# Attention, routed experts and a gated layer in one kernel: the hand-written order also places loads, stores and table reads, and gate stores and decoding move

## The chip, the core and the metric

The kernel runs on one core of a Trainium2 chip. Its engines have queues of their own and run side by side: TensorE (PE; its weight loads are listed as PEld), VectorE (DVE), ScalarE (ACT), GpSimd (POOL) and SyncE (SP), which here only reads table entries and issues DMA transfers. Each engine works through its own instructions in the order in which the program names them; between engines only semaphores hold. The metric is the device time of one execution, in microseconds (us), as the median of several runs.

## What is computed

```python
# attention without a softmax, per batch and head (8 batches, 8 heads, 576 tokens, 64 wide)
kv = einsum('bhsd,bhse->bhde', k, v)
out = einsum('bhsd,bhde->bhse', q, kv)
x = out / sqrt(mean(out * out) + 1e-06) * g_norm       # -> 4608 tokens of 512
# one of 8 experts for each token
logits = x @ w_gate + modality_bias[modality_id]
e_idx, gate_w = argmax(logits), softmax(logits)[e_idx]
x[mask_e] = gate_w * (relu(x[mask_e] @ w1[e]) @ w2[e]) # w1: 512 x 1024, w2: 1024 x 512
# a gated layer; its three weights are given in float64
out = (sigmoid(x @ w_gate2) * (x @ w_val)) @ w_out     # 512 -> 1536 -> 512
```

## The kernel before

**Stages.** First attention, batch by batch (`for b in range(B)`, each with row groups `r` = 0 to 4), which also finds each token's expert; then the expert stage; then the gated layer. Products are made of float32 values split into two parts (`h` for the high part, made by ScalarE, `l` for the rest, made by VectorE), three matmuls for one.

**Attention.** In step (b, r) `emit_out(b - 1, r)` multiplies queries by `kv` on TensorE; ScalarE copies the result out and squares it, VectorE sums the squares (`ssq`). `norm(b - 2)` (L532) makes norms and logits, mostly on VectorE. `choose` (L557) takes the best expert for a pair of batches, `rank` (L573) counts each token's place among its expert's, with ten small matmuls (`rkp`), `lanes` (L603) makes a one-hot table `lo`, `numbers` (L610) multiplies it by token numbers into `lid`: nine activations on ScalarE, or one product on VectorE or GpSimd. Batch 6 is `early`: then `front_items` (L635) reads from the first half of the tokens which two experts have full pairs of tiles (a small matmul `tote`, then some fifteen VectorE operations into `est0`). At b = 7 `front_rows` (L662) finds the row numbers of these two items (VectorE's `se`, 36 small matmuls `phe`, two VectorE operations into `gidx0`) and four indirect gathers on GpSimd fetch their rows.

**Items.** The expert stage works on items of 256 tokens of one expert: items 0 and 1 (`NFRONT` = 2) still inside attention's end, items 2 to 21 in `run`, L1139. An item has four steps j: B(j) is x times a quarter of `w1` (24 matmuls of 256 columns), `h` the relu, D(j) is `h` times a quarter of `w2` (12 matmuls of 512 columns; for items 0 and 1 and odd j 8 matmuls in plain float32, L332).

**The explicit order.** Between attention's loop and `run` stands `ORDER` (L897), a list of names; the program calls `todo[name]()` one after another, which fixes every engine's own sequence. The names: `out0`..`out4` the last batch's products, `o`, `sq`, `ssq` their copies, squares and sums; `n6a n6s n6b`, `n7a n7s n7b` the norms; `S5 S6 S7` the stores of `x` for the last batches, on SP; `rk2p rk2`, `rk3p rk3` ranks, `ln` lanes, `nu2a` and so on numbers (nine activations each); `ch3` the last choice; `totp tot sega segb slots soh php gidx` the tables of all rows (`soh` on VectorE, `php` 72 small matmuls on TensorE, `gidx` the row numbers); `exp` the table of experts `est`; `plx` the exponentials of the logits for the gate (VectorE's difference, ScalarE's Exp with its table load, L832); `plc pld` the scatter's row numbers; `g0 g1` the gathers for items 2 and 3; `nx`, `A`, `xh`, `xl` the norm, transposes and split of gathered rows, by item and tile (`A20` is item 2, tile 0); `w1h4 w1l4`, `w2h4 w2l4` weight splits; `B4`, `h4`, `hl4`, `D4` the products of step 4, which is item 1, j = 0; `L1_j` and `L2_j` the loads of item 1's quarters of `w1` and `w2`; `y0 y1` the results of items 0 and 1.

Item 0, item 1 and item 2 use the same buffer `half0`, so a quarter is loaded for the next item when the split, or the plain D, of the one before has read it. Items 2 and on are loaded only if the expert differs from the one in the buffer; SP reads expert and flag from `est` (L173, L174):

```python
exp=lambda: (experts(), read_item(NFRONT), read_item(NFRONT + 1))
behind = [(f"w1l{NJ1 + j}", j, 0) for j in range(NJ1)] + ...   # item 2's loads, each after the name that frees it
```

**The loop.** `run` walks the 80 steps of items 2 to 21: products, the splits and loads for the items ahead, and beside them `decode`: 28 units of the gated layer's float64 weights, each loaded raw (`d_raw`, 512 KB), and some steps later turned into float32 by ScalarE (`d_e`, L133) and VectorE and stored. Before, unit i was loaded at step 13 i // 6 + 3, its exponent taken two steps later, its store four steps later. `store_gate` (L1075) stores one number for each token to DRAM, in four transfers of runs of four numbers or one; it was called at step 0.

Of the kernel before, what the change touches and what calls it, by code (L numbers as in the profile page):

```python
# [10 lines left out]
F32 = mybir.dt.float32  # L11
# [73 lines left out]
def attention_moe_glu_kernel(  # L85
# [270 lines left out]
    with ExitStack() as st:  # L356
# [250 lines left out]
            lo = lo_t[bp] = wk.tile(bc, BF16, tag="lo", name="lo", bufs=1)  # L607
            nc.vector.tensor_tensor(out=lo, in0=iotab.unsqueeze(1).broadcast_to(bc), in1=lane.unsqueeze(2).broadcast_to(bc), op=ALU.is_equal)

        def numbers(bp, eng, ws=(0, 1)):  # L610

            t0, n, bc, lo = 9 * bp, 9, [128, 9, 128], lo_t[bp]
            for w in ws:
                c = w * NTILE + t0
                if eng is nc.scalar:
                    for t in range(n):
                        nc.scalar.activation(out=lid[:, t0 + t, w, :], in_=lo[:, t, :], func=ACTF.Copy, scale=ct[:, C_TOK + c + t:C_TOK + c + t + 1])
                else:
                    eng.tensor_tensor(out=lid[:, t0:t0 + n, w, :], in0=lo, in1=tokb[:, c:c + n].unsqueeze(2).broadcast_to(bc), op=ALU.mult)
# [74 lines left out]
        for b in range(B):  # L694
            if b < B:
                qc = wk.tile([128, 4, H, D], F32, tag="qc", name="qc", bufs=1)
                nc.scalar.activation(out=qc[:, 0], in_=q_t[b][:, :, 0, :], func=ACTF.Copy)
                emit_kv(b)
            if b == 2:
                make_bias()  # L700
            for r in range(5):
                if b < B and r == 0:
                    nc.scalar.activation(out=qc[:, 1], in_=q_t[b][:, :, 1, :], func=ACTF.Copy)
                    for i in (2, 3):
                        nc.gpsimd.tensor_copy(out=qc[:, i], in_=q_t[b][:, :, i, :])
                if b:
                    emit_out(b - 1, r)
                if b < B:
                    if r == 0:
                        emit_RT(b)  # L710
                    if r < 4:
                        emit_qT((b, r), qc[:, r].rearrange("p h d -> p (h d)"))
                    if b % 2 and r == (4 if b < B - 1 else 0):
                        emit_qT((b, 4), qr_t[b // 2].rearrange("p h d -> p (h d)"))
                    if r == 2:
                        emit_M(b)
                if r == 1:
                    load_kv(b + 2)
                    load_q(b + 2)
                    if b == 0:  # L720
                        load_mod()
                    for i in {5: (1,), 6: (0, 3, 2)}.get(b, ()):
                        store_x(i)
                early = b == B - 2
                if (b, r) in ((4, 1), (5, 4)):
                    rank(b - 4)
                if (b, r) in ((4, 3), (6, 0)):
                    lanes(b // 2 - 2)
                if (b, r) == (4, 3):
                    numbers(0, nc.gpsimd)  # L730
                if early and r == 1:
                    numbers(1, nc.scalar, (0,))
                    numbers(1, nc.vector, (1,))
                if 1 < b < B and r == (2 if early else 1):
                    norm(b - 2)
                if b % 2 and b > 1 and r == 3:
                    choose(b // 2 - 1)
                if early and r == 3:
                    front_items()
                if b == B - 1:  # L740
                    if r == 0:
                        front_rows()
                        for t in range(NFRONT):
                            gather(t)
                    if r == 1:
                        for t in range(NFRONT):
                            read_item(t)
                        ld_scope.close()
                        mw = [mw_scope.enter_context(tc.tile_pool(name="m_wr0", bufs=1, side="right", reuse_waits="tile"))]
                        w1p = w1_scope.enter_context(tc.tile_pool(name="m_w1", bufs=3, side="right", reuse_waits="tile"))  # L750
                        half0 = mw[0].tile([128, 2, KC * F1], F32, tag="half0", name="half0")
                        w1r.append(half0[:, 0].rearrange("p (c f) -> p c f", f=F1))
                        w2r.append(half0[:, 1].rearrange("p (c f) -> p c f", f=DM))
                        for j in range(NJ1):
                            load_w(0, j, 0)
                            load_w(0, j, 1)
                    if r == 4:
                        store_x(B - 4)
# [60 lines left out]
        def experts():  # L819
            nc.vector.tensor_reduce(out=esf[:, 0:NITEM], in_=cmp[0:1], op=ALU.add, axis=AX)  # L820
            nc.vector.tensor_scalar(out=ehi, in0=esf[:, 0:NITEM], scalar1=-1.0, scalar2=float(2 * E), op0=ALU.mult, op1=ALU.add)
            nc.vector.tensor_tensor(out=esf[:, 0:NITEM], in0=esf[:, 0:NITEM], in1=ehi, op=ALU.min)
            nc.vector.tensor_scalar(out=esf[:, 0:NITEM], in0=esf[:, 0:NITEM], scalar1=float(E - 1), scalar2=0.0, op0=ALU.min, op1=ALU.max)
            nc.vector.memset(esf[:, NITEM:NITEM + NFRONT + 2], 1.0)
            nc.vector.tensor_tensor(out=esf[:, NITEM + NFRONT:NITEM + NFRONT + 1], in0=esf[:, NFRONT:NFRONT + 1], in1=front.ep[0:1, 1:2], op=ALU.not_equal)
            nc.vector.tensor_tensor(out=esf[:, NITEM + NFRONT + 2:2 * NITEM], in0=esf[:, NFRONT + 2:NITEM], in1=esf[:, NFRONT:NITEM - 2], op=ALU.not_equal)
            nc.vector.tensor_copy(out=esf[:, 2 * NITEM:], in_=seg[0:1, 17:18])
            nc.vector.tensor_copy(out=est, in_=esf)
# [55 lines left out]
        for bp in (2, 3):  # L884
            steps(f"rk{bp}p rk{bp}", rank_parts(bp))
            todo[f"ln{bp}"] = lambda bp=bp: lanes(bp)
            for w in range(2):
# [4 lines left out]
        steps("plc pld", places())  # L892
        place(ch3=lambda: choose(3), slots=slots, plx=exps, y0=lambda: emit_y(0), y1=lambda: emit_y(1),
              g0=lambda: gather(NFRONT, (0,)), g1=lambda: (gather(NFRONT, (1,)), gather(NFRONT + 1)),
              exp=lambda: (experts(), read_item(NFRONT), read_item(NFRONT + 1)))
        behind = [(f"w1l{NJ1 + j}", j, 0) for j in range(NJ1)] + [(("D" if plain(1, j) else "w2l") + str(NJ1 + j), j, 1) for j in range(NJ1)]
        ORDER = """  # L897
            w1h1 out0 nx01 out1 w2h0 w1h2 o1 nx00 A00 xh00 nx10 A01 n6a w2l0 o0 xl00 nx11 out2 xh01 w1h0 xl01 out3 w1l0 rk2p o3
            sq0 rk2 n6s o2 A11 xh11 B0 L2_0 A10 w2h2 w1l1 w1l2 sq1 ssq0 w1h3 ssq1 h0 S5 ln2 out4 sq2 hl0 o4 B1 ssq2 L1_0 w1l3 sq3
            L1_2 h1 w1h4 B2 sq4 D0 xh10 h2 L1_1 n6b nu2b S6 xl11 xl10 nu2a B3 w2l2 ssq4 ssq3 D1 w1l4 n7a n7s hl2 B4 n7b w2h4 w1h5  # L900
            w1h6 ch3 h4 w1l5 rk3p w1l6 rk3 D2 w2l4 ln3 h3 L1_3 nu3a B5 hl4 totp D3 tot sega segb slots soh B6 D4 exp nu3b php w1h7
            plx gidx w1l7 h5 plc L2_2 h6 L2_1 D5 L2_3 w2h6 B7 w2l6 S7 g0 hl6 g1 nx20 A20 D6 h7 pld w1h8 nx21 xh20 A21 xl20 w1l8
            xh21 D7 xl21 y0 y1
        """.split()
        done = set()
        al.end = NSURE
        for name in ORDER:
            todo[name]()
            done.add(name)
            if "exp" in done:  # L910
                for job in [x for x in behind if x[0] in done]:
                    load_w(NFRONT, *job[1:])
                    behind.remove(job)

    y0p = y0_scope.enter_context(tc.tile_pool(name="y0", bufs=1))
    oidp = y0_scope.enter_context(tc.tile_pool(name="oid", bufs=4))
# [131 lines left out]
    with ExitStack() as st:  # L1048
# [13 lines left out]
        at = {}  # L1062
        for i in range(NEARLY):
            for d, what in ((0, "load"), (2, "exponent"), (2, "words"), (3, "finish"), (4, "store")):
                at.setdefault((13 * i // 6 + 3 + d, what), []).append(i)

        def decode(s, *what):
            for w in what:
# [4 lines left out]
                        getattr(jobs[i], w)()  # L1073

        def store_gate():  # L1075
            gate = dec.tile([128, 512], F32, tag="d_e", name="gate", bufs=1)[:, 0:NTILE]
            nc.vector.tensor_reduce(out=gate, in_=ex, op=ALU.add, axis=AX)
            nc.vector.tensor_scalar(out=gate, in0=gate, scalar1=1e-9, scalar2=None, op0=ALU.add)
            nc.vector.reciprocal(out=gate, in_=gate)
            gatev = gate.rearrange("p (b t) -> p b t", t=9)  # L1080
            for i in range(2):
                d = gate_d.rearrange("(b s) o -> s b o", b=B)[:, i::2, :]
                nc.sync.dma_start(out=d[0:512].rearrange("(p r) b o -> p b (r o)", r=4), in_=gatev[:, :, 4 * i:4 * i + 4])
                nc.sync.dma_start(out=d[512:576, :, 0], in_=gatev[64 * i:64 * i + 64, :, 8])
# [54 lines left out]
        def run(lo, hi):  # L1139
# [18 lines left out]
            for s, (t, j) in enumerate(steps):  # L1158
# [14 lines left out]
                split_w(t, j, 1)  # L1173
                if not plain(t, j):
                    load_w(t + ahead, j, 1)
                if not s and sure:
                    store_gate()
                if s:
                    emit_D(*steps[s - 1])
# [368 lines left out]
```

## Time and profile before

| what | value |
|---|---|
| median of 3 runs | 1498.78 us (1498.56 to 1503.22) |
| the profiled execution | 1500.97 us, its span 1499.2 us |
| mean granted TensorE clock | 0.983 |
| TensorE matmuls busy | 1436.4 us (96% of the span) |
| VectorE busy | 903.6 us (60%) |
| ScalarE busy | 635.3 us (42%) |
| GpSimd busy | 218.0 us (15%) |
| DMA | 360.49 MB, 240 GB/s on average |

Attention takes the first 130 us or so, the explicit order the time until 212, the loop of the expert stage until some 660, the gated layer the rest. Shares over the whole span say little of one stage; the rows below are from the stages that the change touches. In a timeline the first number is the start, the second the duration, in us; x8 are eight instructions drawn together; in brackets stands how long the engine had been idle and what ended that.

### The profile page before, as it was taken

What the parts mean: (1) busy time and instruction counts of PE and PEld (TensorE: products, weight loads), DVE (VectorE), ACT (ScalarE), POOL (GpSimd) and SP (SyncE); (2) the same over time, 40 slices, a digit from 0 to 9 for tenths busy, and PEclk for the clock granted to TensorE, in tenths of its full rate; (3) what the DMA queues carried; (4) which work ended last, traced back from release to release, by engine and by line L of the source; (5) the groups of instructions that cost most, each with busy time, mean ns of one, the idle gap of its engine ahead of it and who ended that gap; (6) DMA issues with size and microseconds to landing.
All of it is one profiled execution on the core that took longest, in us unless ns stands there. A gap on an engine that the chain in (4) does not pass through costs nothing.

```text
span 1499.2 us, 22942 instructions
## 1 busy us (share of the span) xinstructions
PE 1436.4 (96%) x8654; PEld 1227.4 (82%) x8654; DVE 903.6 (60%) x1419; ACT 635.3 (42%) x1010; POOL 218.0 (15%) x302
## 2 busy tenths in 40 slices
PE   6988768999999999999999999999999999999997
PEld 6988557999999999777888887888888888888886
DVE  2568645888888888646886676434553436534342
ACT  3667434556555565745543333222322323212121
POOL 1021031222122121311011101011010100101001
PEclk9999889999999999999999999999999999999999
DMA  9978159988897767849997666556555564646444
GB/s 294 340 278 300 47 198 291 325 285 296 284 295 241 232 214 225 299 163 349 327 348 253 246 216 231 226 196 231 198 219 224 188 254 156 255 159 229 187 159 162
DMA packets 161955, 360.49 MB, mean 240 GB/s; under 512 B 20913, under 2 KB 80561, under 8 KB 154673
## 3 DMA queue, kind: packets, MB, share of 16 engines
q1 hardware_dynamic: 149904, 325.42, 62.5%
q0 software_dynamic: 10432, 32.08, 5.9%
q8 instruction: 70, 1.15, 0.3%
q10 hardware_dynamic: 1504, 1.48, 0.3%
q14 instruction: 45, 0.36, 0.1%
HBM read 302.88 MB, written 68.63 MB: 248 GB/s over the span
## 4 chain that ended last, share of the span: by engine, by line
PE 53%; DMA 4%; issue 1%; POOL 1%; DVE 0%; ACT 0%; POOLq 0%; ACTq 0%
PE gv L1011 10%; PE gv L1013 10%; PE gv L1012 10%; PE ac L1379 6%; PE ac L1377 6%; PE ac L1378 6%; DMA y_d<-y,sidx 3%; PE gv L986 1%; PE gv L985 1%; PE gv L987 1%; PE tr L948 1%; POOL gate_t L939 0%; DMA gate_t<-gate_d,oid 0%; DMA d_raw<-y_d 0%; POOL xg L211 0%
## 5 line engine op out<-in xcount | busy, mean ns | idle before, releaser
L278 PE MATMUL ph<-xh,w1h 128*128 128x256 f32 x576 | 167.9, 292 | 3.5 <-ACT w1h L234 3.5
L1015 DVE TENSOR_TENSOR gm<-u,gv 128x512 f32<-128x512 f32 x96 | 65.9, 686 | 172.4 <-PE gv L1013 169.2
L1379 PE MATMUL ac<-wos,gl 128*128 128x512 f32 x432 | 168.3, 390 | 0.0
L1377 PE MATMUL ac<-wos,gh 128*128 128x512 f32 x432 | 168.2, 389 | 0.0
L1378 PE MATMUL ac<-wos,gh 128*128 128x512 f32 x432 | 168.1, 389 | 0.0
L279 PE MATMUL ph<-xh,w1l 128*128 128x256 f32 x576 | 164.2, 285 | 2.3 <-DVE w1l L236 2.3
L280 PE MATMUL ph<-xl,w1h 128*128 128x256 f32 x576 | 163.9, 284 | 0.0
L1035 ACT ACTIVATE s<-gv 128x512 f32<-128x512 f32 x48 | 28.8, 599 | 262.7 <-issue 205.7
L278 PEld LDWEIGHTS ph<-xh,w1h 128*128 128x128 f32 x576 | 111.0, 193 | 6.2 <-ACT w1h L234 3.8
L279 PEld LDWEIGHTS ph<-xh,w1l 128*128 128x128 f32 x576 | 111.2, 193 | 5.1 <-DVE w1l L236 2.9
L1011 PE MATMUL gv<-half,wt 128*128 128x512 f32 x288 | 112.9, 392 | 0.7 <-DVE u L1015 0.7
L1013 PE MATMUL gv<-half,wt 128*128 128x512 f32 x288 | 112.2, 390 | 0.0
L1012 PE MATMUL gv<-half,wt 128*128 128x512 f32 x288 | 112.1, 389 | 0.0
L280 PEld LDWEIGHTS ph<-xl,w1h 128*128 128x128 f32 x576 | 111.2, 193 | 0.0
L334 PE MATMUL py<-w2h,hh 128*128 128x512 f32 x272 | 107.0, 393 | 0.0
L335 PE MATMUL py<-w2l,hh 128*128 128x512 f32 x272 | 106.7, 392 | 0.0
L336 PE MATMUL py<-w2h,hl 128*128 128x512 f32 x272 | 106.0, 390 | 0.0
L1015 DVE TENSOR_TENSOR s<-u,gv 128x512 f32<-128x512 f32 x48 | 33.0, 688 | 118.3 <-PE gv L1013 118.2
L1361 POOL DMA_INDIRECT out_dram<-ot,to x36 | 37.0, 1029 | 435.7 <-DVE ot L1358 187.1
L1379 PEld LDWEIGHTS ac<-wos,gl 128*128 128x128 f32 x432 | 81.1, 188 | 17.3 <-DVE gl L1346 0.4
L1377 PEld LDWEIGHTS ac<-wos,gh 128*128 128x128 f32 x432 | 81.1, 188 | 17.0 <-ACT gh L1345 0.2
L1378 PEld LDWEIGHTS ac<-wos,gh 128*128 128x128 f32 x432 | 81.1, 188 | 16.9
(310 smaller groups left out, 3349.1 us busy)
## 6 DMA issues: line engine op xcount, KB each, us to landing
wt<-wt_d SPq DMA_DIRECT2D x36, 1536.0 KB
half<-in_moe_w_dram SPq DMA_DIRECT2D x96, 512.0 KB
wos<-wo_d SPq DMA_DIRECT2D x96, 512.0 KB
w1r<-in_moe_w_dram SPq DMA_DIRECT2D x40, 512.0 KB
w2r<-in_moe_w_dram SPq DMA_DIRECT2D x40, 512.0 KB
rows<-w_d SPq DMA_DIRECT2D x24, 512.0 KB
wt<-wt_d SPq DMA_DIRECT2D x48, 256.0 KB
wt_d<-wt SPq DMA_DIRECT2D x12, 1024.0 KB
```

Of the source, the lines that this page charges most:

```text
L278: nc.tensor.matmul(out=o, lhsT=bh[:, c, cs], rhs=hi[:, c, 0:n], start=(c == 0), stop=False)
L279: nc.tensor.matmul(out=o, lhsT=bl[:, c, cs], rhs=hi[:, c, 0:n], start=False, stop=False)
L280: nc.tensor.matmul(out=o, lhsT=bh[:, c, cs], rhs=lo[:, c, 0:n], start=False, stop=(c == KC - 1))
L334: nc.tensor.matmul(out=o, lhsT=hi[:, f, cs], rhs=bh[:, f, :], start=first, stop=False)
L335: nc.tensor.matmul(out=o, lhsT=hi[:, f, cs], rhs=bl[:, f, :], start=False, stop=False)
L336: nc.tensor.matmul(out=o, lhsT=lo[:, f, cs], rhs=bh[:, f, :], start=False, stop=last)
L1011: nc.tensor.matmul(out=o, lhsT=wh, rhs=yh[:, c, :], start=first and c == 0, stop=False, skip_group_check=True)
L1012: nc.tensor.matmul(out=o, lhsT=wh, rhs=yl[:, c, :], start=False, stop=False, skip_group_check=True)
L1013: nc.tensor.matmul(out=o, lhsT=wl, rhs=yh[:, c, :], start=False, stop=last and c == 1, skip_group_check=True)
L1377: nc.tensor.matmul(out=o, lhsT=gh[:, cs], rhs=wh, start=(k == 0), stop=False)
L1378: nc.tensor.matmul(out=o, lhsT=gh[:, cs], rhs=wl, start=False, stop=False)
L1379: nc.tensor.matmul(out=o, lhsT=gl[:, cs], rhs=wh, start=False, stop=(k == NJ - 1))
```

## The change

`numbers` can be given some of its nine tiles: for batch pair 1 ScalarE's nine activations are issued three at a time at r = 0, 1 and 2 of batch 6, not all at r = 1. `choose` of batch pair 1 moves from r = 3 to r = 2 of batch 5. `front_rows` and its four gathers move from r = 0 to r = 1 of batch 7. The explicit order is another one; the reads of the expert table are a step of their own (`RD`), and item 2's eight loads are steps (`L3_j`, `L4_j`), no longer issued by themselves as soon as a buffer is free. In the loop, unit i of the raw weights is loaded at step 25 i // 12 + 5, and the gate is stored at step 12, from `gm0`, a tile that the gated layer's first unit writes later.

```diff
--- before.py
+++ after.py
@@ -607,13 +607,13 @@
             lo = lo_t[bp] = wk.tile(bc, BF16, tag="lo", name="lo", bufs=1)
             nc.vector.tensor_tensor(out=lo, in0=iotab.unsqueeze(1).broadcast_to(bc), in1=lane.unsqueeze(2).broadcast_to(bc), op=ALU.is_equal)
 
-        def numbers(bp, eng, ws=(0, 1)):
+        def numbers(bp, eng, ws=(0, 1), tiles=range(9)):
 
             t0, n, bc, lo = 9 * bp, 9, [128, 9, 128], lo_t[bp]
             for w in ws:
                 c = w * NTILE + t0
                 if eng is nc.scalar:
-                    for t in range(n):
+                    for t in tiles:
                         nc.scalar.activation(out=lid[:, t0 + t, w, :], in_=lo[:, t, :], func=ACTF.Copy, scale=ct[:, C_TOK + c + t:C_TOK + c + t + 1])
                 else:
                     eng.tensor_tensor(out=lid[:, t0:t0 + n, w, :], in0=lo, in1=tokb[:, c:c + n].unsqueeze(2).broadcast_to(bc), op=ALU.mult)
@@ -728,17 +728,18 @@
                     lanes(b // 2 - 2)
                 if (b, r) == (4, 3):
                     numbers(0, nc.gpsimd)
+                if early and r < 3:
+                    numbers(1, nc.scalar, (0,), range(3 * r, 3 * r + 3))
                 if early and r == 1:
-                    numbers(1, nc.scalar, (0,))
                     numbers(1, nc.vector, (1,))
                 if 1 < b < B and r == (2 if early else 1):
                     norm(b - 2)
-                if b % 2 and b > 1 and r == 3:
+                if b % 2 and b > 1 and r == (2 if b == 5 else 3):
                     choose(b // 2 - 1)
                 if early and r == 3:
                     front_items()
                 if b == B - 1:
-                    if r == 0:
+                    if r == 1:
                         front_rows()
                         for t in range(NFRONT):
                             gather(t)
@@ -892,25 +893,21 @@
         steps("plc pld", places())
         place(ch3=lambda: choose(3), slots=slots, plx=exps, y0=lambda: emit_y(0), y1=lambda: emit_y(1),
               g0=lambda: gather(NFRONT, (0,)), g1=lambda: (gather(NFRONT, (1,)), gather(NFRONT + 1)),
-              exp=lambda: (experts(), read_item(NFRONT), read_item(NFRONT + 1)))
-        behind = [(f"w1l{NJ1 + j}", j, 0) for j in range(NJ1)] + [(("D" if plain(1, j) else "w2l") + str(NJ1 + j), j, 1) for j in range(NJ1)]
+              exp=experts, RD=lambda: (read_item(NFRONT), read_item(NFRONT + 1)))
+        for j in range(NJ1):
+            for w in range(2):
+                todo[f"L{w + 3}_{j}"] = lambda j=j, w=w: load_w(NFRONT, j, w)
         ORDER = """
-            w1h1 out0 nx01 out1 w2h0 w1h2 o1 nx00 A00 xh00 nx10 A01 n6a w2l0 o0 xl00 nx11 out2 xh01 w1h0 xl01 out3 w1l0 rk2p o3
-            sq0 rk2 n6s o2 A11 xh11 B0 L2_0 A10 w2h2 w1l1 w1l2 sq1 ssq0 w1h3 ssq1 h0 S5 ln2 out4 sq2 hl0 o4 B1 ssq2 L1_0 w1l3 sq3
-            L1_2 h1 w1h4 B2 sq4 D0 xh10 h2 L1_1 n6b nu2b S6 xl11 xl10 nu2a B3 w2l2 ssq4 ssq3 D1 w1l4 n7a n7s hl2 B4 n7b w2h4 w1h5
-            w1h6 ch3 h4 w1l5 rk3p w1l6 rk3 D2 w2l4 ln3 h3 L1_3 nu3a B5 hl4 totp D3 tot sega segb slots soh B6 D4 exp nu3b php w1h7
-            plx gidx w1l7 h5 plc L2_2 h6 L2_1 D5 L2_3 w2h6 B7 w2l6 S7 g0 hl6 g1 nx20 A20 D6 h7 pld w1h8 nx21 xh20 A21 xl20 w1l8
-            xh21 D7 xl21 y0 y1
+            w2h2 out0 o0 out1 w1h0 sq0 nx01 rk2p A01 nx00 o1 rk2 out2 o2 n6a out3 xh01 A00 w1h1 xh00 nx10 out4 sq1 w1l0 xl01 xl00
+            ssq1 w1h2 w2h0 A10 w1l1 B0 o3 ssq0 o4 xh10 sq3 h0 L1_0 w1l2 w2l2 w1h3 B1 nx11 A11 L1_1 hl0 sq2 S5 w2l0 ln2 B2 w1h4
+            ssq2 n6s w1l3 h2 n6b D0 sq4 xh11 h1 nu2b w1h5 hl2 S6 D1 ssq4 ssq3 w1l4 xl11 B3 n7a xl10 L1_2 n7s B4 n7b ch3 rk3p h3
+            w1l5 rk3 D2 L2_0 L2_2 B5 nu2a totp ln3 h4 S7 w2h4 w2l4 w1h6 nu3b L1_3 hl4 D3 w1h7 tot h5 L2_1 sega segb D4 D5 slots
+            nu3a soh w2h6 w1l6 php w1l7 gidx exp B6 L2_3 RD w2l6 h6 plc hl6 B7 L4_2 L3_2 g0 L3_0 nx20 h7 pld D6 g1 A20 w1h8 nx21
+            A21 xh20 w1l8 L4_0 xh21 xl20 L4_1 D7 y0 y1 xl21 L4_3 plx L3_1 L3_3
         """.split()
-        done = set()
         al.end = NSURE
         for name in ORDER:
             todo[name]()
-            done.add(name)
-            if "exp" in done:
-                for job in [x for x in behind if x[0] in done]:
-                    load_w(NFRONT, *job[1:])
-                    behind.remove(job)
 
     y0p = y0_scope.enter_context(tc.tile_pool(name="y0", bufs=1))
     oidp = y0_scope.enter_context(tc.tile_pool(name="oid", bufs=4))
@@ -1062,7 +1059,7 @@
         at = {}
         for i in range(NEARLY):
             for d, what in ((0, "load"), (2, "exponent"), (2, "words"), (3, "finish"), (4, "store")):
-                at.setdefault((13 * i // 6 + 3 + d, what), []).append(i)
+                at.setdefault((25 * i // 12 + 5 + d, what), []).append(i)
 
         def decode(s, *what):
             for w in what:
@@ -1073,7 +1070,7 @@
                         getattr(jobs[i], w)()
 
         def store_gate():
-            gate = dec.tile([128, 512], F32, tag="d_e", name="gate", bufs=1)[:, 0:NTILE]
+            gate = gm0[:, 0:NTILE]
             nc.vector.tensor_reduce(out=gate, in_=ex, op=ALU.add, axis=AX)
             nc.vector.tensor_scalar(out=gate, in0=gate, scalar1=1e-9, scalar2=None, op0=ALU.add)
             nc.vector.reciprocal(out=gate, in_=gate)
@@ -1173,7 +1170,7 @@
                 split_w(t, j, 1)
                 if not plain(t, j):
                     load_w(t + ahead, j, 1)
-                if not s and sure:
+                if s == 12 and sure:
                     store_gate()
                 if s:
                     emit_D(*steps[s - 1])
```

## Rows read from the trace of the kernel before

**Rows 1.** Windows: busy time and count by engine, granted clock, DMA share, GB/s.

```profile
175.00:200.00 25.00, 8.69 (x43) 5.39 (x39) 4.14 (x12) 3.04 (x4) 1.07 (x2) 0.68 0.35 123
...
300.00:325.00 25.00, 25.00 (x168) 22.93 (x167) 21.19 (x28) 15.11 (x20) 7.34 (x7) 1.00 0.84 272
```

**Rows 2.** Timeline of TensorE, 173 to 212 us: `php`, D5, A20, D7, B8.

```profile
173.29 1.98 PE L812 MATMUL php<-soh,lid 128*128 128x44 bf16 x72
183.58 5.55 PE L332 MATMUL py<-half,hf 128*128 128x512 f32 x8 [8.31 <-DMA half<-in_moe_w_dram]
...
202.95 1.11 PE L255 MATMUL xtp<-ident,xg 128*128 128x128 f32 x4 [10.95 <-DVE xg L244]
...
208.91 3.60 PE L332 MATMUL py<-half,hf 128*128 128x512 f32 x8
211.95 0.68 PE L278 MATMUL ph<-xh,w1h 128*128 128x256 f32 x1
```

**Rows 3.** Waits of SP, 85 to 280 us: total us, times, longest us.

```profile
SPq L173 <- DVE est L828: 26.4, 1, 26.4
SPq L193 <- PE py L332: 24.0, 2, 18.4
```

**Rows 4.** Timeline of SP (S7) and of GpSimd (the first gather for item 2).

```profile
190.48 0.35 SPq L623 DMA_DIRECT2D x_d<-o  x1
...
198.62 0.97 POOL L211 DMA_INDIRECT xg<-x_d,gidx  x1 [43.88 <-DMA x_d<-o]
```

**Rows 5.** Timeline of TensorE: the starts of D0, of B3 and of D1.

```profile
145.99 0.40 PE L334 MATMUL py<-w,hh 128*128 128x512 f32 x1
...
148.74 0.28 PE L278 MATMUL ph<-xh,w1h 128*128 128x256 f32 x1
...
151.61 1.45 PE L332 MATMUL py<-half,hf 128*128 128x512 f32 x3
```

**Rows 6.** Timeline of TensorE, batches 5 to 7 and the order's start: its waits.

```profile
91.16 0.21 PE L581 MATMUL rkp<-oh,ubf 128*128 128x72 bf16 x1 [2.86 <-DVE oh L569]
...
107.22 0.17 PE L637 MATMUL tote<-tot,onesb 128*128 128x8 bf16 x1 [2.54 <-ACT qT L503]
...
118.58 1.09 PE L671 MATMUL phe<-se,lid 128*128 128x4 bf16 x36 [1.68 <-DVE se L667]
...
127.84 2.20 PE L518 MATMUL ops<-R,qT 128*128 128x144 f32 x16 [1.47 <-DVE R L496]
...
135.62 0.38 PE L279 MATMUL ph<-xh,w1l 128*128 128x256 f32 x1 [0.36 <-DVE w1l L236]
```

**Rows 7.** Timeline of ScalarE (numbers, batch 6) and VectorE (end of `norm(5)`).

```profile
102.75 2.74 ACT L617 ACTIVATE lid<-lo,ct 128x128 bf16<-128x128 bf16 x9 [0.40 <-DVE lo L608]
...
126.77 0.20 DVE L555 TENSOR_TENSOR lg<-lg,bias 128x40 f32<-128x40 f32 x1
```

**Rows 8.** Timeline of ScalarE (`plx`) and of TensorE (B9's second matmul).

```profile
169.55 1.28 ACT L832 ACT_TABLE_LOAD   x1
174.03 0.44 ACT L832 ACTIVATE ex<-ex 128x288 f32<-128x288 f32 x1 [3.20 <-DVE ex L831]
...
215.95 0.39 PE L279 MATMUL ph<-xh,w1l 128*128 128x256 f32 x1 [0.45 <-DVE w1l L236]
```

**Rows 9.** Timelines: B of steps 5, 6, 8; SP's first raw load; its exponent.

```profile
239.28 0.28 PE L278 MATMUL ph<-xh,w1h 128*128 128x256 f32 x1
...
242.99 0.82 SPq L127 DMA_DIRECT2D d_raw<-in_moe_w_gate_dram  x1
...
245.26 0.36 PE L278 MATMUL ph<-xh,w1h 128*128 128x256 f32 x1
...
253.43 0.66 ACT L133 ACTIVATE d_e<-d_raw 128x512 f32<-128x512 f32 x1 [7.20 <-DMA w1r<-in_moe_w_dram]
...
264.98 0.28 PE L278 MATMUL ph<-xh,w1h 128*128 128x256 f32 x1
```

**Rows 10.** Window 240 to 245 us, columns as in the first group.

```profile
240.00:245.00 5.00, 5.00 (x33) 4.45 (x32) 3.13 (x4) 2.62 (x4) 2.20 (x2) 1.00 0.86 73
```

## The prediction

> **What bounds the kernel now.** I read the windows first. TensorE is busy all but a few per cent of the span, so only its idle or slow stretches can be won back. Between 175 and 200 us it is busy 8.69 of 25 us at a granted share of 0.68, a mix of the 2.4 and the 1.2 GHz level [rows 1]. The timeline of TensorE names two waits there: after `php` (L812, ends at 175.27) it waits 8.31 us for a weight load before D5, and after B7 10.95 us for gathered rows before A20; the loop's first product B8 starts only at 211.95 [rows 2].
>
> The queue's own waits say why. SP waited 26.4 us in one piece for the table `est` (L173, the reads inside the old `exp` step) and 18.4 us for D5's matmuls (L332) [rows 3]. Behind the first stood L2_1, which D5 needs. Behind the second (L4_1, a load that overwrites what D5 reads) stood S7, the store of the last rows: it was issued at 190.48, the gather followed at 198.62 [rows 4] and A20 at 202.95. So one in-order queue, not an engine, sets this stretch. The end of the kernel hangs on it, since from B8 on TensorE has work almost without a break.
>
> **The order, its main term.** New SP order: L2_0, L2_2, S7, L1_3, L2_1, L2_3, and only then RD and L3/L4. S7 now waits for `n7b` alone, which the choice of the last tokens needs too and which so is done long before `php` can run; it is issued and landed long before the gather; L2_1 is issued before `est` is asked for. What still waits behind RD is L3/L4, for item 2, which `w1h8` wants first.
>
> From the start of `php` to B8 there were 211.95 - 173.29 = 38.66 us [rows 2]. At the high clock the units are: an even D 148.74 - 145.99 = 2.75, a B 151.61 - 148.74 = 2.87 [rows 5], an odd D about 3.5 (3.60 less an overlap) and a transpose group 0.5 (it took 1.11 at the low clock [rows 2]); `php` 1.98 [rows 2]. In the new order D5 stands before `php` and B6 after it, so what follows is `php`, B6, B7, D6, A20, A21, D7: 1.98 + 2 x 2.87 + 2.75 + 2 x 0.5 + 3.5 = 15.0. Cover for the gather: from issue to A20 took 202.95 - 198.62 = 4.33 [rows 2, 4], plus about 1 for `gidx`; B6, B7 and D6 give 8.5. So 3 us of margin. Ahead of `php` VectorE's chain from `totp` to `soh` (some 8 us) runs beside D3, D4 and D5 (9.8).
>
> From B0 to `php` TensorE had 173.29 - 135.26 = 38.0 us of work (B0 restarts at 135.62 after 0.36 of waiting [rows 6]). The new order takes out B6 (2.87) and one `out` (1.1, half of the pair's 2.20 [rows 6]; it moves ahead of B0) and puts in D5 (3.5): 37.5. ScalarE's nine-piece number groups and VectorE's splits fit: summed along the list VectorE reaches `soh` some 3 us before `php` wants it. Thus B8 starts 37.5 + 15.0 = 52.5 after B0.
>
> **The front, which costs.** `front_rows` moves behind step 1 of batch 7, and there behind `norm(5)` on VectorE. Before, TensorE waited 1.68 us for `se` and ran `phe` from 118.58 [rows 6]. Now `se` comes after the second row group's square sum and norm, whose last operation ended at 126.97 when that row group began late [rows 7]; with it starting some 2.5 us earlier I put `se` at 124.4. TensorE, finished with that group at 119.3, waits 5.2 us instead of 1.68 and comes back at the low clock, as after the waits above. That is 3.5 more. The order's first `out`, which before waited 1.47 for VectorE [rows 6], no longer does, but the low clock costs that much again. VectorE has the choice and, by the list, 6.2 us of work to do before B0 and starts on it later too, which I put at 1.1. With 0.2 from the two edits below, B0 comes at 140.1 instead of 135.3: **+4.8**. The gathers, 6 us later, land just before VectorE asks. Bounds: 0 (all hidden) to 8.
>
> Choosing batch pair 1 one step earlier only passes ahead of one 0.7 us reduction, of a 2.86 us wait [rows 6]: -0.7, counted above. Dealing out the numbers gains nothing: the first three now stand on ScalarE ahead of the next row group, and `lo`, which they wait for, is ready only at 102.7 (the nine came then with a 0.40 wait [rows 7]). ScalarE idles 2 us there, and the 2.54 us wait of `tote` for ScalarE [rows 6] splits in two instead of going: +0.9, counted above too.
>
> Together: B8 at 140.1 + 52.5 = 192.6 instead of 211.95, **-19.4**.
>
> **The exponentials at the end.** `plx` now stands behind `y1` on ScalarE, and behind it the split `w1h9`, which B9 needs. Its table load is 1.28 and its exponential 0.44 [rows 8]; before, both lay in ScalarE's idle time under `php`. B9 already waited 0.45 for that split [rows 8], so there is no cover: +1.7, or 3.4 if the clock falls after it; I take **+2.5**. The Trainium skill, page "ScalarE: Activation LUTs", section "What ACT_TABLE_LOAD costs", gives 1283 ns for the load and some 1380 ns for draining the engine before it. The trace shows the first (1.28 us) and no such gap. By the page the term would be about 1.4 us dearer.
>
> **Gate stores and decoding.** At step 0 four stores of single gate values stood on SP, ahead of the first raw unit's load; after them DMA moved 73 GB/s in 240 to 245 us though its engines were 86% busy [rows 10]. That load was issued only at 242.99, and ScalarE's exponent waited 7.20 us for it, with the next weight split behind [rows 9]. The two steps from 245.26 to 264.98 took 19.7 us instead of 2 x 6.05 (the step before took 5.98): 7.6 lost. With no gate stores in the way, and the first load two steps later, the load has a dozen microseconds to spare: **-7.6** (bounds 0 and -7.6). At the other end of the 28 units the last load stays at step 61. The gate stores return at step 12; DMA is then at 0.84 and 272 GB/s, and TensorE is fully busy [rows 1]. A raw load is issued some 17 us before its exponent; the stores take 6 us of SP and about 8 of DMA, so I take 0 there, bounds 0 to 8. Using `gm0` for the gate costs nothing: it is first written long after.
>
> **Sum.** -19.4 + 2.5 - 7.6 = -24.5; for small waits in the new order that I have not seen I give back half a microsecond: -24. The profiled execution took 1500.97 (span 1499.2 and 1.8 around it), so 1477 there; the median of the runs is 1498.78, so I forecast 1475.
>
> **Rivals.**
> *The gate stores hurt again at step 12.* Raw loads now run every other step. The Trainium skill ("DMA: Bandwidth & Descriptors", "Specifications") says that below 512 B the engines read, modify and write; the slow stretch behind the single values agrees (73 GB/s [rows 10]), and moving them does not make them larger. If one raw load is late as before, the 7.6 is only moved: 1482.
> *The gather still ends last.* If VectorE reaches `gidx` 6 to 8 us late, A20 waits 3 to 5 and the low clock takes as much again: 1483 to 1488. Against it: the 3 us margin.
> *The time is given back.* Loads of items 3 and 4 start right after D7 in both kernels; if these, not SP, are what comes late, the loop waits for them: 1494 to 1500.
> *Slower.* After step 12 the missed 8 us of DMA (2.2 MB at 272 GB/s) could be caught up only at the spare rate, about 370 less 272 GB/s: 22 us, or four steps. That makes two raw loads late. It decides from four late loads on: 4 x 7.6 = 30.4 against the 24 and 4.5 more; 1505.
>
> **Chances.** Forecast 0.58 (1467 to 1481), gate stores again 0.20, gather last 0.11, given back 0.06, slower 0.05. About 0.3%, 4.5 us, is what a measurement can tell from no change. Faster takes the first three and a little of the fourth: 0.90; same 0.05; slower 0.05. The range runs from 1467 (front costs hidden: -4.8, and a little) to 1490, which takes in the first three cases.
>
> **What would show it.** In the profile after: no TensorE wait over 2 us between B0 and B8, and a full clock there; SP's wait for `est` with nothing urgent behind it; S7 before 165 us; B8 near 192; a wait of about 5 us before `phe`; a wait of 2 us at B9; no wait at step 6 or 7; DMA slow again for some 8 us near step 12. I am wrong if A20 or D5 still waits, if the front costs more than 8, or if a raw load is late at step 15.

## The result and the profile after

The changed kernel takes 1474.17 us (median of 4 runs, 1472.68 to 1475.85) against 1500.09 us of the kernel before (4 runs, 1498.56 to 1503.22): a ratio of 0.9825, 95% interval 0.9804 to 0.9846. The forecast was 1475 us. The profiled execution took 1474.73 us with a span of 1472.9 us and a granted clock of 0.991; all rows of after below are from it.

First the windows, with the columns of [rows 1]; the last three lie around the gate stores.

```profile
175.00:200.00 25.00, 23.29 (x190) 18.09 (x188) 17.09 (x44) 10.71 (x17) 9.33 (x14) 1.00 0.40 122
...
270.00:275.00 5.00, 5.00 (x35) 4.59 (x35) 4.90 (x9) 3.54 (x5) 1.50 (x2) 1.00 0.82 219
275.00:280.00 5.00, 5.00 (x37) 4.66 (x36) 4.54 (x8) 2.80 (x5) 0.00 (x0) 1.00 0.96 68
280.00:285.00 5.00, 5.00 (x36) 4.59 (x35) 4.05 (x6) 2.58 (x3) 2.18 (x3) 1.00 0.81 131
```

The stretch that had 8.69 us of TensorE work in 25 at a clock of 0.68 [rows 1] now has 23.29 at 1.00. The timeline of TensorE shows why: from `php` over A20 and D7 to B8 no wait is listed, and none before D5 or A20 where [rows 2] has 8.31 and 10.95 us.

```profile
180.17 1.97 PE L813 MATMUL php<-soh,lid 128*128 128x44 bf16 x72
...
190.57 1.03 PE L255 MATMUL xtp<-ident,xg 128*128 128x128 f32 x8
191.44 3.60 PE L332 MATMUL py<-half,hf 128*128 128x512 f32 x8
194.48 0.68 PE L278 MATMUL ph<-xh,w1h 128*128 128x256 f32 x1
```

SP still waits for `est`, but 10.1 us instead of 26.4 (its waits, columns as in [rows 3]), and nothing urgent stands behind: S7 (the first store of `x_d`, on SP's timeline) went at 161.76 and the first gather on GpSimd's at 183.63, released by VectorE's `ehi` and no longer by a store; in [rows 4] these were 190.48 and 198.62.

```profile
SPq L173 <- DVE est L829: 10.1, 1, 10.1
```

```profile
161.76 0.34 SPq L623 DMA_DIRECT2D x_d<-o  x1
...
183.63 0.97 POOL L211 DMA_INDIRECT xg<-x_d,gidx  x1 [21.90 <-DVE ehi L822]
```

The waits in front of the order, on TensorE's timeline, answer to [rows 6]; the last two lines are the first and second matmul of B0.

```profile
89.27 0.24 PE L581 MATMUL rkp<-oh,ubf 128*128 128x72 bf16 x1 [2.27 <-DVE oh L569]
102.27 1.25 PE L518 MATMUL ops<-R,qT 128*128 128x144 f32 x8 [1.15 <-ACT o L521]
105.97 0.17 PE L637 MATMUL tote<-tot,onesb 128*128 128x8 bf16 x1 [1.83 <-ACT qT L503]
122.10 1.12 PE L671 MATMUL phe<-se,lid 128*128 128x4 bf16 x36 [4.85 <-DVE se L667]
131.69 0.19 PE L581 MATMUL rkp<-oh,ubf 128*128 128x72 bf16 x1 [0.92 <-DVE oh L569]
136.72 1.09 PE L255 MATMUL xtp<-ident,xg 128*128 128x128 f32 x4 [4.62 <-DVE xg L244]
142.98 0.37 PE L278 MATMUL ph<-xh,w1h 128*128 128x256 f32 x1
143.18 0.28 PE L279 MATMUL ph<-xh,w1l 128*128 128x256 f32 x1
```

The 4.85 us before `phe` were forecast; the 4.62 us before A01 were not. VectorE and GpSimd tell where they come from: the four gathers of item 0's and 1's rows were issued from 123.90 on, and VectorE got the first rows at 135.93, after 4.29 us of waiting. The DMA issues of 123 to 137 us put the gathers' landing at a median of 9.7 us.

```profile
123.90 1.18 POOL L211 DMA_INDIRECT xg<-x_d,gidx  x1 [2.66 <-DVE gidx L673]
...
135.93 1.29 DVE L244 TENSOR_TENSOR xg<-xg 128x512 f32<-128x512 f32 x2 [4.29 <-DMA xg<-x_d,gidx]
```

```profile
xg<-x_d,gidx POOLq DMA_INDIRECT x4, 9.7
```

In the windows the clock is 0.50 in 120 to 125 and in 135 to 140 us, that is at 1.2 GHz, after each of these two long waits. DMA is full between them, and its share is 0.05 once the rows have landed.

```profile
120.00:125.00 5.00, 2.90 (x44) 2.90 (x45) 2.23 (x8) 0.00 (x0) 1.31 (x2) 0.50 1.06 362
125.00:130.00 5.00, 5.00 (x38) 4.99 (x38) 1.07 (x3) 3.33 (x6) 2.93 (x4) 0.83 1.03 342
130.00:135.00 5.00, 1.18 (x17) 0.90 (x15) 1.50 (x6) 3.69 (x6) 0.00 (x0) 0.85 0.97 399
135.00:140.00 5.00, 3.28 (x14) 3.31 (x15) 3.86 (x15) 0.23 (x1) 0.00 (x0) 0.50 0.05 18
```

At the end of the order ScalarE (first two lines) loads `plx`'s table and takes the exponential just before the split `w1h9`; B9 (TensorE, last two) waits for it and for the `w1l` made from it, 1.94 us together, where [rows 8] has 0.45.

```profile
196.23 1.28 ACT L833 ACT_TABLE_LOAD   x1
197.53 0.45 ACT L833 ACTIVATE ex<-ex 128x288 f32<-128x288 f32 x1
...
198.97 0.38 PE L278 MATMUL ph<-xh,w1h 128*128 128x256 f32 x1 [1.06 <-ACT w1h L234]
200.23 0.39 PE L279 MATMUL ph<-xh,w1l 128*128 128x256 f32 x1 [0.88 <-DVE w1l L236]
```

Behind it TensorE waits for nothing until the gated layer. The steps that began at 239.28, 245.26 and 264.98 in [rows 9] begin here as follows, and the last two lines are SP's last gate store with the raw load behind it.

```profile
223.55 0.28 PE L278 MATMUL ph<-xh,w1h 128*128 128x256 f32 x1
...
229.54 0.36 PE L278 MATMUL ph<-xh,w1h 128*128 128x256 f32 x1
...
241.29 0.28 PE L278 MATMUL ph<-xh,w1h 128*128 128x256 f32 x1
...
273.28 0.70 SPq L1081 DMA_DIRECT2D gate_d<-gm  x1
274.02 0.61 SPq L127 DMA_DIRECT2D d_raw<-in_moe_w_val_dram  x1
```

Two steps take 241.29 - 229.54 = 11.75 us instead of 19.72: the stall is gone. The slow DMA came with the stores to 275 to 280 us (68 GB/s at a share of 0.96) and held nobody up.

### The profile page after: what moved, and what is told of

It is laid out like the page before. It is cut to its first block, busy times and chain, and to the rows that moved or that the text cites. A ratio compares the mean times of both kernels' runs of the same rounds, so it can differ in the third digit from the quotient of the medians.

```text
span 1472.9 us, 22928 instructions
## 1 busy us (share of the span) xinstructions
PE 1428.3 (97%) x8654; PEld 1221.6 (83%) x8654; DVE 903.6 (61%) x1419; ACT 635.6 (43%) x1010; POOL 217.2 (15%) x302
## 3 DMA queue, kind: packets, MB, share of 16 engines
q8 instruction: 70, 1.15, 0.3%
q10 hardware_dynamic: 1504, 1.48, 0.3%
## 4 chain that ended last, share of the span: by engine, by line
PE 54%; DMA 1%; issue 0%; DVE 0%; ACT 0%; POOL 0%; POOLq 0%; SPq 0%; ACTq 0%
PE gv L1008 10%; PE gv L1010 10%; PE gv L1009 10%; PE ac L1376 6%; PE ac L1374 6%; PE ac L1375 6%; PE gv L984 1%; PE gv L982 1%; PE gv L983 1%; PE tr L945 1%; DMA rows<-w_d 1%; POOL out_dram L1358 0%; ACT wt L970 0%; DVE u L1012 0%; POOLq L1541 0%
```

## The experiments

All ratios are to the kernel before, with its 95% interval.

**One part of the change alone (e1 to e3; 4, 4 and 10 runs).** e1 is the kernel before with four items moved on SP's list and nothing else:

```diff
-  slots soh B6 D4 exp nu3b php w1h7
+  slots soh B6 D4 S7 L2_2 L2_1 L2_3 exp nu3b php w1h7
-  plx gidx w1l7 h5 plc L2_2 h6 L2_1 D5 L2_3 w2h6 B7 w2l6 S7 g0
+  plx gidx w1l7 h5 plc h6 D5 w2h6 B7 w2l6 g0
```

> The kernel before, with S7, L2_2, L2_1 and L2_3 moved ahead of the old exp step, so that on SP nothing but item 2's loads stands behind the table reads; every other engine's sequence is as before. If the in-order queue set the stretch: no wait of TensorE before D5 or A20, B8 at about 189 us instead of 211.95, the stall of step 7 as before: 1477 to 1480 us. If the new sequence of products and splits is what gained: a wait before A20 stays, B8 at 200 or later, 1490 us or more.

Measured: 1478.66 us, 0.9851 (0.9833 to 0.9870). TensorE's timeline has no wait before D5 or A20, the loop starts at 191.54, B9 waits 0.45 as before, and the stall of step 7 is still there, 3.97 and 1.26 us:

```profile
191.54 0.68 PE L278 MATMUL ph<-xh,w1h 128*128 128x256 f32 x1
...
195.54 0.39 PE L279 MATMUL ph<-xh,w1l 128*128 128x256 f32 x1 [0.45 <-DVE w1l L236]
...
235.12 0.58 PE L278 MATMUL ph<-xh,w1h 128*128 128x256 f32 x1 [3.97 <-ACT w1h L234]
236.96 0.58 PE L279 MATMUL ph<-xh,w1l 128*128 128x256 f32 x1 [1.26 <-DVE w1l L236]
```

Four names moved in one list bring 22 of the 26 us, with every other engine's own order as it was.

e2 is the kernel before with the gate edit alone:

```diff
-  gate = dec.tile([128, 512], F32, tag="d_e", name="gate", bufs=1)[:, 0:NTILE]
+  gate = gm0[:, 0:NTILE]
-  if not s and sure:
+  if s == 12 and sure:
```

> The kernel before, with the gate stores at step 12 and nothing else. If the gate stores' slow DMA stretch made the first raw load late: no TensorE wait at step 7, 1492 to 1493 us (7.6 less), and none at step 15. If the early first load itself is the cause: the wait at step 7 stays, 1500 us. If the stores only move the stall: a wait of some 3 us near step 15, 1498 to 1500 us.

Measured: 1493.1 us, 0.9947 (0.9929 to 0.9965). The waits of 8.8 and 10.7 us before D5 and A20 stay, the stall goes, and nothing takes its place at step 12 or behind, though a raw load is due every other step there and the windows behind its stores show the slow DMA again:

```profile
295.00:300.00 5.00, 5.00 (x34) 4.46 (x33) 4.06 (x6) 2.70 (x5) 0.62 (x1) 1.00 0.83 57
300.00:305.00 5.00, 5.00 (x34) 4.51 (x33) 4.97 (x7) 3.77 (x5) 4.22 (x4) 1.00 1.03 360
```

The edit also takes the gate out of `d_e`, the one buffer that the first exponent writes too, so the exponent could have waited for the stores to have read it. The trace of the kernel before excludes that: the stores' packets of 16 and 4 bytes were over by 237.3 us, the 4 KB packets of the raw load ran only from 249.6 to 252.8, and the exponent began at 253.43 [rows 9]. So it waited for the raw load, although the row names a weight load.

e3 is the kernel before with the later decoding alone; the gate stores stay at step 0:

```diff
-  at.setdefault((13 * i // 6 + 3 + d, what), []).append(i)
+  at.setdefault((25 * i // 12 + 5 + d, what), []).append(i)
```

> The kernel before, with the raw loads at steps 25 i // 12 + 5 and nothing else; the gate stores stay at step 0. If the gate stores are the cause, the first raw load is still issued late (about 250 us), its exponent waits 1 to 4 us instead of 7.2, and 3 to 6 us are won: 1494 to 1497 us. If the time given to the first load is the cause: no wait left, 1492 to 1493 us.

Measured: 1495.67 us, 0.9968 (0.9951 to 0.9984), with single runs from 1490 to 1500. The stall shrinks to waits of 0.37 and 1.45 us. So either edit alone goes most of the way, and the gate stores' move goes all of it.

**S7 behind the table read (e7, four runs).** The rival to e1's reading is that the new sequence of the engines matters and SP's list little. e7 is the kernel after with one store moved back:

```diff
-  ln3 h4 S7 w2h4 w2l4
+  ln3 h4 w2h4 w2l4
-  exp B6 L2_3 RD w2l6
+  exp B6 L2_3 RD S7 w2l6
```

> The kernel after, with S7 moved on SP's list to right behind RD, the read of the table est; all else as in the kernel after. Theory (a store that stands behind the table read holds the gather, and TensorE with it): est is read at about 184.6, S7 goes then, lands some 4 to 8 us later, and A20 waits 5 to 8 us and runs on at the low clock for a few us: 8 to 11 us more, 1482 to 1485. Rival (the new order of the engines, not that of SP's queue, brought the gain): S7's place costs no more than 2 us, 1474 to 1476.

Measured: 1485.97 us, 0.9911 (0.9881 to 0.9941), 11.8 us over the kernel after and a microsecond over the theory's range. The timelines show the whole chain again: GpSimd's gather released by the store, TensorE's waits before A20 and A21, and B8 ten microseconds late; the window of 195 to 200 us has the clock at 0.50.

```profile
191.87 0.97 POOL L211 DMA_INDIRECT xg<-x_d,gidx  x1 [31.60 <-DMA x_d<-o]
```

```profile
196.17 1.12 PE L255 MATMUL xtp<-ident,xg 128*128 128x128 f32 x4 [6.91 <-DVE xg L244]
198.77 1.12 PE L255 MATMUL xtp<-ident,xg 128*128 128x128 f32 x4 [1.48 <-DVE xg L244]
199.68 5.39 PE L332 MATMUL py<-half,hf 128*128 128x512 f32 x8
204.50 0.68 PE L278 MATMUL ph<-xh,w1h 128*128 128x256 f32 x1
```

**The front (e4 and e9, four runs each).** e4 is the kernel after with front rows and gathers back at step 0 of batch 7:

```diff
-  if r == 1:
+  if r == 0:
       front_rows()
```

> The changed kernel, with front_rows and its gathers back at step 0 of batch 7. If the later place costs what the trace shows (a wait of 4.85 us before phe, then 4.62 us for the gathered rows, both at the low clock after): these two waits shrink to about 1.7 and 0 us, B0 comes 6 to 8 us earlier, 1467 to 1468 us. If the later place is the better one, because TensorE is not held by phe: 1475 to 1478 us.

Measured: 1474.5 us, 0.9826 (0.9807 to 0.9844): no gain, so that theory fell. TensorE's wait before `phe` shrank to 1.48 us and that before A01 to 1.14, but ScalarE's timeline (first two lines) shows what came up behind them: `w2h2`, the first ScalarE item of the new list, waits 6.14 us for its weight load with `o0` behind it, and TensorE (third line) waits 3.39 us for that.

```profile
133.94 1.06 ACT L234 ACTIVATE w<-half 128x1024 fp32r<-128x1024 f32 x1 [6.14 <-DMA half<-in_moe_w_dram]
134.91 0.63 ACT L521 ACTIVATE o<-ops 128x576 f32<-128x576 f32 x1
...
135.59 4.29 PE L518 MATMUL ops<-R,qT 128*128 128x144 f32 x16 [3.39 <-ACT o L521]
```

In the kernel after the later front rows hid most of this: counted from `rkp`, ScalarE comes to `w2h2` 4.7 us later there (at 130.10), and it ran without a wait. e9 adds to e4 that `w2h2` moves down the list:

```diff
-  w2h2 out0 o0 out1 w1h0
+  out0 o0 out1 w1h0
-  w1h2 w2h0 A10
+  w1h2 w2h0 w2h2 A10
```

> The kernel after with the front rows back at step 0 of batch 7, as in e4, and with the split w2h2 moved from the head of the list to behind w2h0. Theory (in e4 the front rows' gain was lost to w2h2, which waited 6.14 us on ScalarE for its weight load and held o0 behind it): ScalarE goes on with o0, out waits no more than 1.5 us for it, B0 starts 3 to 5 us earlier than in e4 (141.9), and the time falls from 1474.5 to 1470 to 1471.5. Rival (the loads of item 0 and the gathers together fill DMA, and whatever stands first waits): xh00 or w1h1 waits in its place, B0 stays within 1 us of 141.9, and the time at 1474.

Measured: 1469.28 us, 0.9795 (0.9773 to 0.9817). ScalarE reaches `o0` at 127.47, TensorE's waits there are 0.77 us and less, and B0 starts at 134.65 (e4: 141.94; 2.0 of the difference lie before `rkp`). The interval overlaps with that of the kernel after, so the gain rests on the waits that went away, more than on the medians.

```profile
127.47 0.65 ACT L521 ACTIVATE o<-ops 128x576 f32<-128x576 f32 x1 [1.43 <-PE ops L518]
...
134.65 0.36 PE L278 MATMUL ph<-xh,w1h 128*128 128x256 f32 x1
```

**The exponentials (e5, four runs).** The kernel after with `plx` early:

```diff
-  gidx exp B6
+  gidx exp plx B6
-  xl21 L4_3 plx L3_1 L3_3
+  xl21 L4_3 L3_1 L3_3
```

> The kernel after, with the exponentials of plx back beside exp, ahead of y0 and y1 on ScalarE. Theory (plx behind y1 costs the 1.28 us table load and the 0.44 us exponential in front of w1h9, 1.75 us between B8 and B9): the table load lies in ScalarE's idle time again, the wait of B9 falls from 1.94 us in two pieces to about 0.45, and the time from 1474.2 to about 1472.5. Rival (ScalarE is as full around exp, and the table load there only delays a split that B6 or B7 waits for): the 1.7 us comes back as a wait between php and B8, and the time stays at 1474.

Measured: 1471.57 us, 0.9806 (0.9786 to 0.9827). No TensorE wait came up between `php` and B8; B9's wait is 0.44 us, and from B8 to that matmul it is 197.20 - 193.21 = 3.99 us, as before the change (in time alone the interval overlaps with that of the kernel after):

```profile
197.20 0.38 PE L279 MATMUL ph<-xh,w1l 128*128 128x256 f32 x1 [0.44 <-DVE w1l L236]
```

**The numbers (e6, five runs).** The kernel after with the nine number operations together at step 1 of batch 6:

```diff
-  if early and r < 3:
-      numbers(1, nc.scalar, (0,), range(3 * r, 3 * r + 3))
   if early and r == 1:
+      numbers(1, nc.scalar, (0,))
```

> The kernel after, with the nine number operations of pair 1 together again at step 1 of batch 5 instead of three in each of three steps. Theory (dealing them out splits ScalarE's wait for lo and tote's wait for ScalarE in two and costs 0.8 us): the two TensorE waits of 1.15 and 1.83 us become one of about 2.5, and the time falls by 0.5 to 0.8 us, to 1473.5. Rival (what is won there is lost again at the w2h2 weight load in the front): 1474.2.

Measured: 1472.59 us, 0.9813 (0.9794 to 0.9832), an interval that overlaps with that of the kernel after. The two waits of 1.15 and 1.83 us became one of 2.54, which is 0.44 us less. But that is within what one kernel differs from run to run: dealt out, the waits are 2.98 us in e4, 2.40 in e9 and 2.31 in e5 and e7; together, they are 2.53 to 3.14 in e1, e2, e3 and e10. So no cost of the dealing is shown. Its B0 came earlier by more than 0.44, but its gathers landed in 8.3 us instead of 9.7, and one profile can't tell whether that is the edit's doing: inconclusive.

**Without the new engine sequence (e10), and the best of both (e11, e12).** e10 (four runs) is e1, e2 and e3 in one: the kernel before with the four SP items, the gate edit and the later decoding.

> The kernel before with its own engine order, front rows, numbers and plx, and three edits alone: S7 and L2_2, L2_1, L2_3 moved ahead of the table reads on SP (e1), the gate stores at step 12 (e2) and the later decoding (e3). Theory (the two waits on SP and the decoding stall are the whole gain, and the rest of the new order costs some 3 us in the front and at plx): 1478.7 less the 7 to 7.9 us that the gate edit gave alone, 1471 to 1472, faster than the kernel after by 2 to 3 us. Rival (the new sequence of the engines carries part of the gain): 1474 or more, not faster than the kernel after.

Measured: 1468.84 us, 0.9793 (0.9771 to 0.9815), 2 us below the theory's range. B8 starts at 187.47, TensorE's longest wait from there to 576 us is 0.7 us. e12 (five runs) adds the earlier choice:

```diff
-  if b % 2 and b > 1 and r == 3:
+  if b % 2 and b > 1 and r == (2 if b == 5 else 3):
```

> The kernel e10 (before, with the SP moves, the gate stores at step 12 and the later decoding), and batch pair 1's choose one step earlier. Theory (choose then passes one reduction on VectorE): the rkp wait falls from 2.86 to about 2.3 us, and the time from 1468.8 by 0.6, to 1468.2, too little to tell from e10. Rival (the tote wait of ScalarE behind it takes the 0.6 us up): 1468.8.

Measured: 1468.26 us, 0.9778 (0.9757 to 0.9798); the wait of `rkp` fell from 2.86 to 2.26 us. e11 (five runs) is the kernel after with e9's, e5's and e6's edits:

> The kernel after with what the runs so far found dear taken back: front rows at step 0 of batch 7 and w2h2 behind w2h0 (as in e9), plx beside exp (as in e5), and the nine number operations together again at step 1 of batch 5. Theory (the three costs lie at three places and add up): 1469.3 less 1.7 to 2.6 for plx less about 0.8 for the numbers, 1466 to 1467. Rival (with B0 earlier the split or the gather behind is late, and the gain at plx is lost to it): 1469.

Measured: 1467.74 us, 0.9771 (0.9751 to 0.9791). B0 starts at 132.72, B8 at 186.98, and B9's wait is 0.45; but `tote` waits 2.7 us, so the numbers gave nothing. The intervals of e11 and e12 lie below that of the kernel after (0.9804 to 0.9846): both beat both kernels, and by these runs one can't be told from the other.

## Why the prediction was right

The time was right within a microsecond, and the mechanism was right as well. One term came out larger than forecast, and differences that no step foresaw made up for it, so the closeness of the fit is in part luck. Split at the same points, in the profiled executions:

- *Start to `rkp`.* The row at 91.16 [rows 6] is now at 89.27: 0.6 of that is the shorter wait (2.86 to 2.27; predicted 0.7), the other 1.3 lie before anything that the change touches. The same code has `rkp` at 89.09 to 92.69 in e1, e2, e3 and e10, so this can be the execution alone.
- *`rkp` to B0, the term that was mis-sized.* From `rkp` to B0's second matmul it is 143.18 - 89.27 = 53.91 us against 135.62 - 91.16 = 44.46: +9.45 in this pair. The prediction had +5.5 here (its +4.8 with the 0.7 of the choice taken out). Its wait of 5.2 us before `phe` came as 4.85. What failed is the sentence that the gathers "land just before VectorE asks": they landed 9.7 us after issue, beside item 0's weight loads, and A01 waited 4.62 us, with a second stretch of low clock behind it; that is most of the missing four. The low clock behind `phe` was forecast to eat the 1.47 us saved at `out`. In this pair it adds little, since the profile of before has it too, as the same eight matmuls show (before, then after):

```profile
119.53 2.27 PE L518 MATMUL ops<-R,qT 128*128 128x144 f32 x8
...
123.08 2.27 PE L518 MATMUL ops<-R,qT 128*128 128x144 f32 x8
```

  Part of the +9.45 is chance of these two executions. With the front of the kernel before, the stretch took 44.97 to 46.54 us in e1, e2, e3 and e10, so 44.46 was the shortest; with that of the kernel after it took 52.33 in e5 and 50.44 in e7, where A01 waited 2.3 and 1.35 us, so 53.91 was the longest. So the term is some 4 to 9.5 us, 6.6 between the means, depending among other things on when the gathers land; that is nearer to the forecast than this pair alone makes it look. The +0.9 for the dealt numbers is not borne out (e6). The prediction also took the earlier place of the front rows for free; e4 showed that with this list it isn't, since `w2h2` stands at the list's head and its load is not there; e9, with both edits, is 4.9 us faster by the medians.
- *B0 to B8.* 194.48 - 142.98 = 51.5 us, predicted 52.5, with `php` to B8 14.3 for 15.0. From B0's second matmul to B8 the kernel before took 211.95 - 135.62 = 76.33 and this one 51.30: -25.0 for a predicted 24.2. e1 and e7 show from both sides that the place of stores and loads on SP does this.
- *`plx`.* From B8 to B9's second matmul 5.75 us instead of 4.00: +1.75, predicted +2.5; the clock did not fall (1.00 in the windows of 195 to 205 us), with the wait in two pieces of about 1 us. The Trainium skill ("ScalarE: Activation LUTs", "What ACT_TABLE_LOAD costs") adds a drain of the engine to the 1283 ns of the load. The trace after does not show it: the copy of `y` that ends at 196.22 is followed by the load at 196.23, and that by the exponential at 197.53.
- *Gate stores and decoding.* 11.75 us instead of 19.72 for the two steps: -8.0, predicted -7.6; e2 alone gave 1493.1 us for 1500.99. The rival that they hurt again at step 12 fell: DMA did drop to 68 GB/s, and no wait followed. The Trainium skill's rule on pieces under 512 B ("DMA: Bandwidth & Descriptors", "Specifications") agrees in so far as the slow stretch moved with the stores; no run shows the read-modify-write itself. What decided the time here is who waited for DMA just then.
- *The rest.* -1.3 - 0.6 + 9.45 - 25.0 + 1.75 - 8.0 = -23.7; the spans differ by 26.3. The last 2.6 us are at the seam to the gated layer, where TensorE's wait for `yr` fell from 2.3 to 1.3 us and a low clock behind it went away. It was 1.5 us in e1, 1.6 in e10, and 2.3 and 2.2 in e11 and e12, so it goes with the execution and not with this change.

With the front as mis-sized and nothing else, the forecast would have been some 4 us too low; the start-up and the seam gave those back. The profiled pair gained 26.3 us for a forecast 24; that the median came within a microsecond of 1475 is also because the kernel before, 1498.78 us when the forecast was made, has a median of 1500.09 over four runs.

The new engine sequence shows no gain of its own: e10, without it, is 5 us faster than the kernel after by the medians (the intervals overlap), and e11, which has it without `w2h2` at its head, the later front rows, the late `plx` and the dealt numbers, can't be told from e12.

## What to carry to other kernels

Read an in-order issue queue as a list of its own: one wait on it (here 26 us for a table) is paid by whatever urgent stands behind, and moving four names ahead of it brought more than reordering every engine. When a step is moved off a wait, look at what was hidden under that wait: the first item of a new list may need a transfer that has not landed. Slow, small stores need not be made faster if they can be put where no one waits for DMA in the next ten microseconds.

## What the runs showed of the hardware

- The four indirect gathers of the front land 7 to 10 us after issue (medians: 6.8 in e1 to 9.7 in the kernel after) while weight loads fill DMA (in the kernel after a share of 0.97 to 1.06, 342 to 399 GB/s); the gather of 183.63, in a window with a share of 0.40, was in use by 187.24. The same code landed in 7.9, 8.0, 8.3 and 9.7 us in four kernels (medians of e5, e7, e6 and after), and TensorE's wait for the rows of A01 was 2.3 us, 1.35, none and 4.62.
- After four stores of gate values, in runs of four numbers or one (last issued at 273.28), DMA was at a share of 0.96 and moved 68 GB/s for 5 us, then 131; in e2 it was 57 GB/s. It was back at 360 or more some ten microseconds later (382 in 285 to 290 us; in e2 360 in 300 to 305).
- TensorE ran on at 1.2 GHz after waits of 4.85, 4.62 and 6.91 us, but kept 2.4 GHz through waits of 1.06 and 0.88 us one behind the other. After the same wait of 1.68 us before `phe` the next eight matmuls took 2.27 us in the profile of before and 1.23 in e2, e3 and e10: the length of the wait alone did not decide it.
